# The last pair of heads after all five head fours, wider turned keys, and four more unread matmuls at the end of a decode kernel

## The chip, the core and the metric

The kernel runs on one core of one Trainium2 chip. The metric is the time of one execution on the device in microseconds (us), the median over several runs. Beside it there is the profile of one execution, whose clock starts at its first instruction; all points of time below are counted from there.

## What is computed

One decode step of a gated mix of two branches, for a batch of 8 with one new token each and a width of 576. Branch A is attention with cached keys and values (32 heads of width 128, 4096 positions); branch B is a small MLP.

```python
g = _sigmoid((x * gate_w).sum(-1, keepdims=True))
q = (x @ wq).reshape(B, Sq, H, Dh).transpose(0, 2, 1, 3)
scores = jnp.einsum("bhqd,bhkd->bhqk", q, k_cache) * (Dh ** -0.5)
p = _softmax(scores, axis=-1)
o = jnp.einsum("bhqk,bhkd->bhqd", p, v_cache)
a = o.transpose(0, 2, 1, 3).reshape(B, Sq, H * Dh) @ wo
b = _gelu(_layernorm(x) @ w1 + b1) @ w2 + b2
return g * a + (1 - g) * b
```

The keys and values are 268 MB each, in bf16, and everything is read once.

## The kernel before, in words

The work is cut into 32 groups (`NG`), each of 8 heads (`HB`) of one batch row. A group's keys lie over 128 partitions as 8 heads by 16 stretches of 256 positions. `scores` multiplies them by the query on VectorE (`mult`, L496), sums over the head width on TensorE against an identity matrix (L507 and, with weights that are already loaded, `held`, L180) and on VectorE (`reduce`, L515); `softmax` follows; `pv` (L556) multiplies probabilities by values, `evict` (L568) brings the sums to SBUF, and `gather` (L573) picks each head's rows out of them with the selection matrix `selO`, fp32, 8 columns wide. The order of each engine's instructions is written out by hand: the text order of the calls is the order in each engine's queue. The groups 1 to 30 are hardware loops on TensorE and VectorE; the start and the last group are written out straight. SyncE's queue issues all the large loads.

The change lies in the last group alone (`last`, 31), after its scores. Its values come in ten loads, `load_v_last` with the sizes of `V_LAST`; `v_part[i]` holds each one's pair of heads, its range and its landing.

- Parts 0 to 2 hold positions 0 to 159 of each stretch of 256, for all heads; `pv` works on them as on any group.
- Parts 3 to 9 hold the other 96 positions, ordered by pairs of heads: parts 3 and 4 are pairs 0 and 1 with 24 keys each per partition (`KW`), parts 5 and 6 are pair 2 with 16 and 8, and parts 7, 8 and 9 are the last pair with 8 each (256 KB a part).

`pv_turned` (L756) works on parts 3 to 9 with the roles turned: the values are the weights (128x128, one load each) and the probabilities the moving columns. For pairs 0 to 2 it streams 8 columns and adds onto what `gather` left in the bank `qb_ps`; for the last pair it streams 2 columns into the bank `o_ps[0]`. `norm_turned` (L763, result `v_A`) divides the heads of pairs 0 to 2 and writes them to `OT_sb`, which the projection reads; `norm_first` (L768) does so for the last pair's first positions; `norm_wide` (L772, result `v_B`) adds the last pair's turned part. `a_proj` projects with `wo`: per head four matmuls of 144 columns, one for each quarter of the output width, on 32 columns of the array each (`quarters`, L619). "Five fours" are five heads with four such matmuls each; the projection of this last group has 8 heads. L856 combines both branches, and one DMA writes the result. `keep_busy(n)` (L743 for the first, L180 for the others) issues n matmuls of 512 columns whose result nobody reads; they wait for nothing that is still under way at their place.

Before the change, the end of the last group ran in this order on TensorE: gather; parts 3, 4, 5, 6; part 7; projection of 4 heads; part 8; projection of 1 head; part 9; projection of 1 head; and, after `norm_wide`, of the last 2 heads.

Of the kernel before, what the change touches and what calls it, by code (L numbers as in the profile page):

```python
# [14 lines left out]
H = 32  # L15
# [7 lines left out]
HB = 8  # L23
# [11 lines left out]
TQ = 4  # L35
# [7 lines left out]
class Stream:  # L43
# [10 lines left out]
    def op(self, engine, fn, waits=(), dma=None, side=0):  # L54

        rec = [fn, [w for w in waits if w is not None], None, dma, (engine, side)]
        self.ops[engine].append(rec)
        if dma is not None:
            return ("dma", *dma)
        return ("op", engine, rec)  # L60
# [81 lines left out]
def bass_gated_mix__mha_block_cached__mixer_channel_mlp__decode_kernel(  # L142
# [18 lines left out]
    op = S.op  # L161

    def aside(engine, fn, waits=()):
        return op(engine, fn, waits, side=1)

    def pstride(t):
        return t[tuple([slice(None)] * len(t.shape))].ap[0][0]

    def view(t, offset, shape):
        ap = []  # L170
        stride = 1
        for n in reversed(shape[1:]):
            ap.insert(0, [stride, n])
            stride *= n
        return bass.AP(tensor=t, offset=offset, ap=[[pstride(t), shape[0]]] + ap)


    def held(e, out, lhsT, rhs, stop):

        return e.add_instruction(mybir.InstMatmult(  # L180
            name=nc.get_next_instruction_name(), engine=mybir.EngineType.PE,
            ins=[e.lower_ap(rhs), e.lower_ap(lhsT)], outs=[e.lower_ap(out)],
            start_tensor_calc=False, stop_tensor_calc=stop, tile_size=(128, 128), tile_position=(0, 0),
            ldweights=False))
# [15 lines left out]
    p1 = sb("p1", [128, 2, CT, DH], BF16)  # L200
# [36 lines left out]
    PW = view(p1, 2 * (FW + 3 * QN), [128, HB // 2, HB, (B * NHG - 8)])  # L237
# [9 lines left out]
    selO = sb("selO", [128, TQ, HB], F32)  # L247
# [19 lines left out]
    O_sb = sb("O_sb", [128, TQ, DH], F32)  # L267
# [5 lines left out]
    o_ps = bank[2:4]  # L273
    qb_ps = bank[4]
# [70 lines left out]
    NP = HB // 2  # L345
    KW = (NTT - T_ALL) // 4
# [21 lines left out]
    last = NG - 1  # L368
# [18 lines left out]
    def blank(ps):  # L387
# [17 lines left out]
    t = op("vector", lambda e: e.tensor_reduce(out=stat[:, 0:1], in_=x_sb, axis=AX.X, op=ALU.add), [ld_x])  # L405
    t1 = op("vector", lambda e: e.tensor_tensor_reduce(out=junk, in0=x_sb, in1=x_sb, scale=1.0, scalar=0.0,
                                                       op0=ALU.mult, op1=ALU.add, accum_out=stat[:, 1:2]))
    t = op("vector", lambda e: e.tensor_scalar(out=stat[:, 2:3], in0=stat[:, 0:1], scalar1=1.0 / D, scalar2=None,
                                               op0=ALU.mult), [t])
    t = op("vector", lambda e: e.tensor_tensor(out=stat[:, 3:4], in0=stat[:, 2:3], in1=stat[:, 2:3], op=ALU.mult), [t])  # L410
    t = op("vector", lambda e: e.scalar_tensor_tensor(out=stat[:, 6:7], in0=stat[:, 1:2], scalar=1.0 / D,
                                                      in1=stat[:, 3:4], op0=ALU.mult, op1=ALU.subtract), [t, t1])
# [30 lines left out]
    t = op("vector", lambda e: e.reciprocal(out=stat[:, 7:8], in_=stat[:, 5:6]), [a_sqrt])  # L443
# [8 lines left out]
    for half in range(2):  # L452
        for h in range(4):
            for kt in range(NKT):
                o = tr_ps[half][32 * h:32 * h + B, :]
                at = (kt * SK + half * (SK // 2) if kt < NKF else NKF * SK) + h * DH
                r = bass.AP(tensor=VB, offset=at, ap=[[pstride(VB), 128], [4 * DH, 4], [1, DH]])
                xi = kt if kt < NKF else NKF + half
                p_Q = aside("tensor", lambda e, o=o, r=r, kt=kt, xi=xi: e.matmul(
                    o, lhsT=xT_sb[:, xi, :], rhs=r, start=(kt == 0), stop=(kt == NKT - 1)),  # L460
# [8 lines left out]
    a_qb, v_mult, v_red, p_sum, v_nm, a_exp, v_P, p_pv, a_ev, p_oz, v_norm, v_rs, p_z, v_rz = ({} for _ in range(14))  # L469
# [99 lines left out]
                                                      func=ACT.Copy), [p_pv[n], p_oz.get(n - 1)])  # L569

    def gather(n, o, stop=True):
        for tt in range(TQ):
            p_oz[n] = op("tensor", lambda e, tt=tt: e.matmul(  # L573
                o, lhsT=O_sb[:, tt, :], rhs=selO[:, tt, :], start=(tt == 0), stop=(tt == TQ - 1 and stop)),
                [a_ev[n], v_norm.get(n - 1), c_selO] if tt == 0 else ())

    def norm(n):
# [37 lines left out]
    def quarters(t, n, j, w, first, stop, waits, end=aside):  # L615

        lhsT = bass.AP(tensor=t, offset=j, ap=[[pstride(t), 128], [n // BS, 32]])
        for i in range(4):
            last = (end if i == 3 else aside)("tensor", lambda e, i=i: e.matmul(  # L619
                y_ps[32 * i:32 * i + 32, 0:QN], lhsT=lhsT, rhs=w[:, i * QN:(i + 1) * QN], start=first, stop=stop),  # L620
                waits if i == 0 else ())
        return last
# [73 lines left out]
    def a_proj(h0, h1, normed):  # L696
        for h in range(h0, h1):
            st["p_a"] = quarters(OT_sb, H, h, wo_sb[:, h, :], h == H - HB, h == H - 1,
                                 [a_O[NG - 2], *normed, st["ld_wo3"], st["a_bx"]] if h == h0 else ())
# [38 lines left out]
    def keep_busy(n):  # L738

        for i in range(n):  # L740
            r = wo_sb[:, i, 0:512]
            if i == 0:
                fn = lambda e, r=r: e.matmul(tr_ps[1][:, :], lhsT=ident[:, :], rhs=r, start=True, stop=(n == 1))  # L743
            else:
                fn = lambda e, r=r, i=i: held(e, tr_ps[1][:, :], ident[:, :], r, i == n - 1)
            aside("tensor", fn, [v_red[last, NC - 1], st["ld_wo"]] if i == 0 else ())

    def pv_turned(n, i):
        g, t0, t1, land = v_part[i]
        for t in range(t0, t1):  # L750
            v = VL[:, T_ALL + g * KW + t, :]
            if g < NP - 1:
                o, p, start, stop = qb_ps[:, 0:HB], PW[:, g, :, t], False, (g, t) == (NP - 2, KW - 1)
            else:
                o, p, start, stop = o_ps[0][:, 0:2], PW[:, g, HB - 2:HB, t], t == 0, t == KW - 1
            p_oz[n] = op("tensor", lambda e, o=o, v=v, p=p, start=start, stop=stop: e.matmul(  # L756
                o, lhsT=v, rhs=p, start=start, stop=stop), [land, st["v_PW"]] if t == t0 else ())

# [3 lines left out]
    def norm_turned(n):  # L762
        return op("vector", lambda e: e.tensor_tensor(  # L763
            out=OT_b[:, n % B, H - HB:H - 2], in0=qb_ps[:, 0:HB - 2], in1=rz[:, 0:HB - 2], op=ALU.mult), [p_oz[n], v_rz[n]])

    def norm_first(n):

        v_norm[n] = op("vector", lambda e: e.tensor_tensor(  # L768
            out=X2[:, :], in0=qb_ps[:, HB - 2:HB], in1=rz[:, HB - 2:HB], op=ALU.mult), [p_oz[n], v_rz[n]])

    def norm_wide(n):
        return op("vector", lambda e: e.tensor_tensor(  # L772
            out=OT_b[:, n % B, H - 2:H], in0=o_ps[0][:, 0:2], in1=X2[:, :], op=ALU.add), [p_oz[n], v_norm[n]])
# [5 lines left out]
    for n in range(NG):  # L779
# [40 lines left out]
        pv(n - 1, v_land[n - 1], 0, NTT)  # L820
        evict(n - 1)
        gather(n - 1, oz_ps[:, 0:HB])
        if n < last:
            load_v(n)
# [15 lines left out]
    pv(last, v_part[2][3], *v_part[2][1:3])  # L840
    evict(last)
    keep_busy(3)
    gather(last, qb_ps[:, 0:HB], False)
    for i in range(3, 7):
        pv_turned(last, i)
    v_A = norm_turned(last)
    norm_first(last)
    pv_turned(last, 7)
    a_proj(H - HB, H - HB + 4, [v_A])
    pv_turned(last, 8)  # L850
    a_proj(H - HB + 4, H - HB + 5, [v_A])
    pv_turned(last, 9)
    v_B = norm_wide(last)
    a_proj(H - HB + 5, H - 2, [v_A])
    a_proj(H - 2, H, [v_B])
    t = op("vector", lambda e: e.scalar_tensor_tensor(  # L856
        out=out_sb[0:QP, :], in0=y_ps[0:QP, 0:QN], scalar=g4[0:QP, 0:1], in1=bmg_sb[0:QP, :],
        op0=ALU.mult, op1=ALU.add), [st["p_a"], st["g_bmg"]])
# [44 lines left out]
```

## Time and profile before

| | |
|---|---|
| median of 3 runs | 1297.49 us (1297.48 to 1297.62) |
| the profiled execution, its own time | 1297.77 us |
| its span, first to last instruction | 1295.7 us |
| mean granted TensorE clock | 0.829 of full |
| TensorE busy (matmul) | 58% of the span |
| VectorE busy | 66% |
| HBM read | 556.96 MB, 430 GB/s over the span |

In the profile, PE is TensorE's matmuls, PEld its weight loads, DVE is VectorE, ACT ScalarE, POOL GpSimd, and SP (SPq) SyncE's queue. "L756" is line 756 of the kernel. A line of the timeline gives the start, the length from the first start to the last end of a row of like instructions, engine, line, operation, operands, shapes and count; in brackets is how long the engine sat idle before and what ended that. PEclk is the granted TensorE clock, 1.00 being full.

### The profile page before, as it was taken

The numbers are of one execution on the slowest core, as the hardware profiler recorded it, in microseconds if no ns is written. First come the engines' busy times: TensorE is split into PE (matmuls) and PEld (weight loads), VectorE is DVE, ScalarE is ACT, GpSimd is POOL, SyncE is SP. The second block draws the span as 40 slices with busy tenths as digits, with TensorE's granted clock in tenths as the row PEclk, the third lists the DMA queues.
The fourth block names the chain that finished last, engine by engine and source line by source line (L and its number), as shares of the span: only waits on it lengthen the run. The fifth ranks groups of instructions, "written<-read, shape, count | busy, mean of one in ns | idle before, by whom it ended". The sixth has DMA issues, their size and how long they took to land.

```text
span 1295.7 us, 10767 instructions
## 1 busy us (share of the span) xinstructions
PE 745.8 (58%) x5042; PEld 155.4 (12%) x3247; DVE 851.9 (66%) x1083; ACT 69.7 (5%) x165; POOL 16.7 (1%) x29
## 2 busy tenths in 40 slices
PE   3865556555556555556555546645546655546657
PEld 1521111011111001111001111001111001111003
DVE  3656667766668766668766667766667776667772
ACT  3100000000000000000000000000000000000001
POOL 0010000000000000000000000000000000010000
PEclk8867898777889778888877888877789878789877
DMA  9999999999999999999999999999999999999998
GB/s 406 426 444 427 437 433 429 443 427 433 435 431 441 427 431 439 429 441 427 429 443 429 437 431 429 443 427 433 435 431 441 427 431 439 431 437 429 431 428 333
DMA packets 13283, 557.12 MB, mean 430 GB/s; under 512 B 1608, under 2 KB 2648, under 8 KB 3800
## 3 DMA queue, kind: packets, MB, share of 16 engines
q1 hardware_dynamic: 12996, 556.94, 99.6%
q8 instruction: 7, 0.11, 0.0%
q10 hardware_dynamic: 276, 0.04, 0.0%
q14 instruction: 4, 0.03, 0.0%
HBM read 556.96 MB, written 0.01 MB: 430 GB/s over the span
## 4 chain that ended last, share of the span: by engine, by line
DMA 68%; DVE 19%; PE 9%; issue 3%; SPq 0%; DVEq 0%
DMA KR<-in_A_k_cache_dram 67%; DVE p L496 17%; PE psb L180 7%; DVE s_sb L515 2%; DMA KR<-in_A_v_cache_dram 2%; PE psb L507 2%; SPq L285 0%; DVEq L135 0%; PE psb L619 0%; PE psb L756 0%; DVE out_sb L856 0%
## 5 line engine op out<-in xcount | busy, mean ns | idle before, releaser
L496 DVE TENSOR_TENSOR p<-KR,q_n 128x4096 bf16<-128x4096 bf16 x256 | 582.5, 2286 | 230.5 <-DMA KR<-in_A_k_cache_dram 230.5
L180 PE MATMUL psb<-p,ident 128*128 128x512 bf16 x1792 | 487.5, 418 | 0.0
L507 PE MATMUL psb<-p,ident 128*128 128x512 bf16 x256 | 111.7, 436 | 501.3 <-DVE p L496 501.2
L515 DVE TENSOR_REDUCE s_sb<-psb 128x32 f32<-128x512 f32 x256 | 175.2, 684 | 92.0 <-PE psb L180 92.0
L507 PEld LDWEIGHTS psb<-p,ident 128*128 128x128 bf16 x256 | 26.3, 103 | 951.2 <-DVE p L496 951.0
L556 PE MATMUL psb<-VB,P 128*32 128x512 bf16 x1984 | 112.7, 380 | 1.8 <-DMA VB<-in_A_v_cache_dram 1.8
L544 DVE TENSOR_SCALAR P<-E,own 128x256 bf16<-128x256 bf16 x248 | 51.4, 282 | 84.3 <-ACT E L541 84.3
L483 ACT ACTIVATE q_n<-q_bc 128x128 bf16<-128x128 bf16 x32 | 9.9, 309 | 867.7 <-DVE p L496 867.6
L556 PEld LDWEIGHTS psb<-VB,P 128*32 128x32 bf16 x1984 | 50.3, 97 | 49.8 <-DMA VB<-in_A_v_cache_dram 2.0
L573 PE MATMUL psb<-selO,O_sb 128*128 128x8 f32 x256 | 33.8, 258 | 21.8 <-ACT O_sb L568 21.8
L573 PEld LDWEIGHTS psb<-selO,O_sb 128*128 128x128 f32 x256 | 31.1, 191 | 37.8 <-ACT O_sb L568 37.8
L568 ACT ACTIVATE O_sb<-psb 128x512 f32<-128x512 f32 x32 | 19.1, 597 | 171.4 <-PE psb L556 171.4
L594 PE MATMUL psb<-yT_sb,KR 128*128 128x8 bf16 (+1 forms) x216 | 19.6, 229 | 0.0
L594 PEld LDWEIGHTS psb<-yT_sb,KR 128*128 128x128 bf16 (+1 forms) x216 | 18.4, 165 | 2.7 <-issue 1.4
L563 PEld LDWEIGHTS psb<-rs,ones 128*128 128x128 f32 x64 | 12.1, 190 | 45.8 <-issue 44.4
L541 ACT ACTIVATE E<-s_sb,mD 128x256 bf16<-128x256 f32 x32 | 16.0, 500 | 9.4 <-DVE mD L540 9.4
L648 POOL TENSOR_TENSOR Q<-Q,b 125x144 f32<-125x144 f32 x1 | 1.1, 1072 | 1067.3 <-DMA b<-in_B_b_dram 1067.3
L532 DVE TENSOR_REDUCE mA<-s_sb 128x1 f32<-128x256 f32 x32 | 13.4, 420 | 1.1
L547 DVE TENSOR_REDUCE es<-E 128x1 f32<-128x256 bf16 x32 | 13.2, 412 | 0.0
L488 ACT ACTIVATE OT_sb<-O_n 128x8 bf16<-128x8 bf16 x31 | 6.5, 208 | 83.2 <-DVE O_n L579 83.2
L578 DVE RECIPROCAL rz<-psb 128x8 f32<-128x8 f32 x31 | 6.2, 201 | 5.5 <-PE psb L573 5.5
L563 PE MATMUL psb<-rs,ones 128*128 128x8 f32 x64 | 9.2, 216 | 0.5 <-DVE O_n L579 0.5
(105 smaller groups left out, 134.1 us busy)
## 6 DMA issues: line engine op xcount, KB each, us to landing
KR<-in_A_k_cache_dram SPq DMA_DIRECT2D x2, 4096.0 KB, 27.2
VB<-in_A_v_cache_dram SPq DMA_DIRECT2D x1, 5376.0 KB, 20.8
VB<-in_B_w_dram SPq DMA_DIRECT2D x1, 5184.0 KB, 39.8
KR<-in_B_w_dram SPq DMA_DIRECT2D x1, 4608.0 KB, 43.2
VB<-in_A_wq_dram SPq DMA_DIRECT2D x1, 4096.0 KB, 12.5
KR<-in_A_v_cache_dram SPq DMA_DIRECT2D x2, 2048.0 KB, 13.9
KR<-in_A_wo_dram SPq DMA_DIRECT2D x1, 3456.0 KB, 24.8
VB<-in_A_v_cache_dram SPq DMA_DIRECT2D x1, 2816.0 KB, 38.8
```

What stands on the lines that cost most here:

```text
L180: return e.add_instruction(mybir.InstMatmult(name=nc.get_next_instruction_name(), engine=mybir.EngineType.PE, ins=[e.lower_ap(rhs), e.lowe ...
L496: v_mult[n, c] = op("vector", lambda e: e.tensor_tensor(out=p1[:, par, :, :], in0=k, in1=qb, op=ALU.mult), [k_land[n, s], a_q[n], p_sum.ge ...
L507: fn = lambda e, r=r: e.matmul(tr_ps[par][:, :], lhsT=ident[:, :], rhs=r, start=True, stop=False)
L515: v_red[n, c] = op("vector", lambda e: e.tensor_reduce(out=s_sb[:, at:at + CT], in_=tr_ps[par][:, :].rearrange("p (t c) -> p t c", c=CH), ...
L532: t = op("vector", lambda e: e.tensor_reduce(out=mA[:, 0:1], in_=s_sb[:, :], axis=AX.X, op=ALU.max), [v_red[n, NC - 1], c_mA])
L541: a_exp[n] = op("scalar", lambda e: e.activation(out=E[:, :], in_=s_sb[:, :], func=ACT.Exp, bias=mD[:, 0:1], scale=1.0), [v_nm[n], v_P.get ...
L544: v_P[n] = op("vector", lambda e, h=h: e.tensor_scalar(out=(P if n < NG - 1 else P_last)[:, :, h, :], in0=E[:, :].rearrange("p (q t) -> p ...
L556: p_pv[n] = op("tensor", lambda e, o=o, tq=tq, at=at, v=v: e.matmul(o, lhsT=(P if n < last else P_last)[:, tq, :, :].rearrange("p h t -> p ...
L563: p_z[n] = op("tensor", lambda e: e.matmul(oz_ps[:, HB:2 * HB], lhsT=ones[:, :], rhs=rs[:, :], start=True, stop=True), [v_rs[n], v_norm.ge ...
L568: a_ev[n] = op("scalar", lambda e: e.activation(out=O_sb[:].rearrange("p t d -> p (t d)"), in_=o_ps[n // last][:, :], func=ACT.Copy), [p_p ...
L573: p_oz[n] = op("tensor", lambda e, tt=tt: e.matmul(o, lhsT=O_sb[:, tt, :], rhs=selO[:, tt, :], start=(tt == 0), stop=(tt == TQ - 1 and stop)),
L594: st["p_up"] = (op if end else aside)("tensor", lambda e, w=w, o=o, kt=kt: e.matmul(o, lhsT=w, rhs=yT_sb[:, kt, :], start=(kt == 0), stop= ...
```

## The change

`gather` and `pv_turned` build the moving operand by hand, with a step of 0 that repeats the same columns: the last gather and the turned parts of pairs 0 to 2 stream their 8 columns four times (32 columns), those of the last pair their 2 columns sixteen times. The repeated columns land in columns of the bank that nobody reads. For all other groups the gather's operand is what it was. Two calls of `keep_busy(2)` are put in, behind part 3 and behind part 4. The projection of five heads comes right behind `norm_turned`, and parts 7, 8 and 9 follow it back to back; the projections of the last three heads stay behind them.

```diff
     def gather(n, o, stop=True):
+        k = o.shape[1] // HB
         for tt in range(TQ):
-            p_oz[n] = op("tensor", lambda e, tt=tt: e.matmul(
-                o, lhsT=O_sb[:, tt, :], rhs=selO[:, tt, :], start=(tt == 0), stop=(tt == TQ - 1 and stop)),
+            r = bass.AP(tensor=selO, offset=tt * HB, ap=[[pstride(selO), 128], *([[0, k]] if k > 1 else []), [1, HB]])
+            p_oz[n] = op("tensor", lambda e, tt=tt, r=r: e.matmul(
+                o, lhsT=O_sb[:, tt, :], rhs=r, start=(tt == 0), stop=(tt == TQ - 1 and stop)),
                 [a_ev[n], v_norm.get(n - 1), c_selO] if tt == 0 else ())
...
+    WS = 32
+
     def pv_turned(n, i):
+
         g, t0, t1, land = v_part[i]
+        p1s = pstride(p1)
         for t in range(t0, t1):
             v = VL[:, T_ALL + g * KW + t, :]
             if g < NP - 1:
-                o, p, start, stop = qb_ps[:, 0:HB], PW[:, g, :, t], False, (g, t) == (NP - 2, KW - 1)
+                o, h0, start, stop = qb_ps[:, 0:WS], 0, False, (g, t) == (NP - 2, KW - 1)
             else:
-                o, p, start, stop = o_ps[0][:, 0:2], PW[:, g, HB - 2:HB, t], t == 0, t == KW - 1
+                o, h0, start, stop = o_ps[0][:, 0:WS], HB - 2, t == 0, t == KW - 1
+            p = bass.AP(tensor=p1, offset=PW.offset + (g * HB + h0) * KW + t,
+                        ap=[[p1s, 128], [0, WS // (HB - h0)], [KW, HB - h0]])
...
     keep_busy(3)
-    gather(last, qb_ps[:, 0:HB], False)
-    for i in range(3, 7):
-        pv_turned(last, i)
+    gather(last, qb_ps[:, 0:WS], False)
+    pv_turned(last, 3)
+    keep_busy(2)
+    pv_turned(last, 4)
+    keep_busy(2)
+    pv_turned(last, 5)
+    pv_turned(last, 6)
     v_A = norm_turned(last)
     norm_first(last)
-    pv_turned(last, 7)
-    a_proj(H - HB, H - HB + 4, [v_A])
-    pv_turned(last, 8)
-    a_proj(H - HB + 4, H - HB + 5, [v_A])
-    pv_turned(last, 9)
+    a_proj(H - HB, H - HB + 5, [v_A])
+    for i in range(7, 10):
+        pv_turned(last, i)
     v_B = norm_wide(last)
     a_proj(H - HB + 5, H - 2, [v_A])
     a_proj(H - 2, H, [v_B])
```

## The prediction

> **What bounds the kernel now.** I read the page first, for its span and the shares of the chain that ended last; then the end of that chain, in order of time; then the timeline of the last ten microseconds, since the diff touches nothing earlier.
>
> ```profile
> span 1295.7 us, 10767 instructions
> ...
> DMA 68%; DVE 19%; PE 9%; issue 3%; SPq 0%; DVEq 0%
> ```
>
> ```profile
> 1269.20 21.12 DMA KR<-in_A_v_cache_dram
> 1290.32 0.05 issue
> 1290.36 0.37 PE psb L756 x8
> ```
>
> Two thirds of the span are transfers. The loads run ahead of the engines up to the last group, so all that this change can move is what lies behind the last values' landings. The chain says where that begins: part 7 (issued at 1269.20) lands at 1290.32, its eight turned matmuls start at 1290.36, 0.04 us behind the landing, and from there TensorE is named without a break.
>
> ```profile
> 1286.01 0.95 PE L573 MATMUL psb<-selO,O_sb 128*128 128x8 f32 x8
> 1286.82 0.78 PE L756 MATMUL psb<-p,KR 128*128 128x8 bf16 x24
> 1287.80 0.80 PE L756 MATMUL psb<-p,KR 128*128 128x8 bf16 x24 [0.19 <-DMA KR<-in_A_v_cache_dram]
> 1289.09 1.03 PE L756 MATMUL psb<-p,KR 128*128 128x8 bf16 x24 [0.49 <-DMA KR<-in_A_v_cache_dram]
> 1289.73 0.29 PEld L756 LDWEIGHTS psb<-p,KR 128*128 128x128 bf16 x8 [0.15 <-DMA KR<-in_A_v_cache_dram]
> 1290.16 0.17 DVE L763 TENSOR_TENSOR OT_sb<-psb,rz 128x6 bf16<-128x6 f32 x1 [9.82 <-PE psb L756]
> 1290.67 0.70 PE L619 MATMUL psb<-KR,OT_sb 128*32 128x144 bf16 x16
> 1291.31 0.37 PE L756 MATMUL psb<-p,KR 128*128 128x2 bf16 x8
> 1291.61 0.35 PE L619 MATMUL psb<-KR,OT_sb 128*32 128x144 bf16 x4
> 1291.89 0.37 PE L756 MATMUL psb<-p,KR 128*128 128x2 bf16 x8
> 1292.19 0.79 PE L619 MATMUL psb<-KR,OT_sb 128*32 128x144 bf16 x12
> 1292.30 0.16 DVE L772 TENSOR_TENSOR OT_sb<-psb,X 128x2 bf16<-128x2 f32 x1 [1.91 <-PE psb L756]
> 1292.51 0.21 PEld L619 LDWEIGHTS psb<-KR,OT_sb 128*32 128x32 bf16 x8 [0.18 <-DVE OT_sb L772]
> 1293.03 0.37 DVE L856 SCALAR_TENSOR_TENSOR out_sb<-psb,g,Q 125x144 bf16<-125x144 f32 x1 [0.57 <-PE psb L619]
> 1293.42 0.69 SPq L285 DMA_DIRECT2D out_dram<-out_sb  x1
> ```
>
> Parts 4, 5 and 6 wait for their landings (the brackets: 0.19, 0.49, 0.15 us), so up to 1290.16 the transfers set the pace. Parts 8 and 9 wait for nothing in brackets; they stand in TensorE's queue behind the projection. Part 9 starts at 1291.89. When did its values land?
>
> ```profile
> 1270.49 6.70 SPq L285 DMA_DIRECT2D KR<-in_A_v_cache_dram  x1
> KR<-in_A_v_cache_dram SPq DMA_DIRECT2D x1, 256.0 KB, 21.1
> ```
>
> This is the last of the ten loads: 1270.49 + 21.1 gives 1291.59. TensorE took it up 0.30 us later; that is the room for a new order. The TensorE clock is the second thing, read in stretches of 3.41 us whose borders are where the clock changes.
>
> ```profile
> core 0: us, PE busy (x), PEclk, DMA share, GB/s
> 1268.68:1272.09 3.41, 1.63 (x28) 1.00 0.81 344
> 1272.09:1275.51 3.42, 3.41 (x64) 1.00 1.01 426
> 1275.51:1278.92 3.41, 2.21 (x26) 1.00 1.00 420
> 1278.92:1282.33 3.41, 2.70 (x30) 0.50 0.98 410
> 1282.33:1285.74 3.41, 3.35 (x23) 0.50 1.01 414
> 1285.74:1289.16 3.42, 2.74 (x61) 1.00 1.02 388
> 1289.16:1292.57 3.41, 3.10 (x76) 0.50 0.23 87
> ```
>
> ```profile
> 1278.08 1.12 PE L556 MATMUL psb<-KR,p 128*32 128x512 bf16 x16
> L756 PE MATMUL psb<-p,KR x96: 165/175/193, 1286.8 to 1292.1; 128*128 128x8 bf16 x72, 128*128 128x2 bf16 x24
> ```
>
> In the first fence the clock is full or half, and it is half from 1289.16 to the end, where nothing hides TensorE any more. The two rows of the second fence are used below: where the wide matmuls of one stretch begin, and how long one turned matmul is (0.175 us).
>
> **The change part by part. The order.** `norm_turned` still starts at 1290.16, if part 6 isn't late (below), and ends at 1290.33. The projection's weight load follows VectorE by 0.05 us (L772 ends at 1292.46, the load starts at 1292.51), so the five heads start at 1290.38. Part 7, landed at 1290.32, now stands behind that wait, and parts 8 and 9 behind it; 0.06 us of TensorE are lost, at no cost, since the last landing comes later. Length of five heads at half clock: sixteen matmuls take 0.64 us up to the first of part 8 (1290.67 to 1291.31), four take 0.28 (1291.61 to 1291.89), so a head is 0.12 and twenty take 0.76, to 1291.14. Sixteen turned matmuls: 24 in 0.78 with a last one of 0.175 long means 0.026 from start to start, so parts 7 and 8 take 0.42, to 1291.56. Part 9 can't start before 1291.59 + 0.04 = 1291.63. So the new order just meets the last landing at half clock, with 0.07 us to spare, and by 0.4 us more at full clock. Part 9 then takes 0.37 as before, to 1292.00, and `norm_wide` starts 0.04 us behind (1291.89 + 0.37 = 1292.26 against 1292.30): at 1292.04 where it was 1292.30. **Term one: -0.26 us.** What is late next is the landing itself. No DMA and no instruction of ScalarE, GpSimd or SyncE changes its place, and the output's DMA still follows L856. The sixth head's four matmuls start beside `norm_wide` (0.21 us from its start to the next weight load) and stay hidden, as now.
>
> **The clock at the end.** Behind `norm_wide` lie 0.73 us (1292.30 to 1293.03): 0.21 to the weight load, two heads, the last matmul's own length, and VectorE.
>
> ```profile
> L619 PE MATMUL psb<-VB,hT_sb x144: 225/324/337, 73.7 to 77.7; 128*32 128x144 bf16 x144
> L619 PE MATMUL psb<-KR,OT_sb x32: 324/330/338, 1290.7 to 1292.6; 128*32 128x144 bf16 x32
> ```
>
> The first row is the MLP's down projection, the same shape; its shortest matmuls, 225 ns, are those behind a change to full clock, its median, 324, those at half. At full clock the last matmul is 0.105 shorter (330 to 225 ns), and the head in front of it takes 0.06 in place of 0.12. **Term two: -0.165 us, if the clock is full there.** Is it? Count how long columns stream in a stretch, at 0.228 us per 512 (below), 0.014 per 32. In 1268.68:1272.09 all 28 matmuls are wide ones, 1.63 us, and the clock stays full. In 1275.51:1278.92 the wide ones begin at 1278.08 and stream for 0.84, the others carry 8 columns: about 0.9, and it falls. In 1285.74:1289.16 an older unread matmul streams for 0.26, and 60 of 8 columns for 0.2: 0.46, and it falls, though the engine is counted busy for 2.74. So the border is between 0.9 and 1.63 us of streaming. The change makes this stretch 0.26 + 0.11 (gather) + 51 x 0.014 = 0.71 + 4 x 0.228 = 0.91: 2.0 us. It should stay full up to 1292.57, past the start of the last heads at about 1292.25.
>
> [...]
>
> **Wider streams.** No row has 32 columns behind a 128-column bf16 load; the nearest on both sides:
>
> ```profile
> 1249.21:1249.61 0.40, 0.40 (x9) 1.00 1.44 547
> 1249.21 0.40 PE L670 MATMUL psb<-Q,shift 128*128 128x64 bf16 x8
> 1279.16 0.50 PE L729 MATMUL psb<-E,q_bc 128*128 128x24 bf16 x12
> 1271.87 3.64 PE L556 MATMUL psb<-VB,P 128*32 128x512 bf16 x64 [1.78 <-DMA VB<-in_A_v_cache_dram]
> ```
>
> With 0.175 for the last one's length again, 64 columns at full clock are (0.40 - 0.175) / 7 = 0.032 apart, and 24 columns at half (0.50 - 0.175) / 11 = 0.030. Loads overlap streams in both, so I take about 0.027, as with 8 columns, and a cost of nothing; by 0.030 part 9 would be 0.03 longer. The other end is load and stream one after the other: 0.026 + 0.014 = 0.040 at full clock, 0.053 at half. In part 9 alone that is 7 x 0.014 = 0.10 or 7 x 0.027 = 0.19 us on the path; in parts 3 to 6 the waits for landings take it at full clock. Below nothing it can't be: more columns are streamed through the same loads. [...]
>
> **The unread matmuls.** At full clock 512 columns cost 0.228 (64 in four columns of the array, 16 rows of 0.228 in 3.64). Part 3's last one starts at 1287.43; two unread ones run from 1287.46 to 1287.91, part 4 starts 0.11 late and is through at 1288.55, two more end at 1289.01, and part 5 waits until 1289.09 anyway. [...] Without that cover (half clock, below) they cost 0.43 each.
>
> **Sum.** -0.26 - 0.165 = -0.42 us. The profiled execution took 1297.77 (1295.7 of span and 2.1 around it), so 1297.35 for it; it lies 0.28 over the median of the runs, 1297.49, and the median becomes 1297.07.
>
> **The rivals.** *The clock isn't moved* in the last stretch, because unread columns don't count for it or because the grid of 3.41 us falls elsewhere in other executions, which one profile can't show. For it: the rows give a border, not a rule. Against: 2.0 us is above every stretch that fell. [...] The order still pays: -0.26, 1297.23.
>
> *Slower: at half clock, the wide streams don't overlap their weight loads.* The place is parts 7 to 9, which no longer have the projection between them. The five heads end at 1291.14, sixteen at 0.053 end at 1291.99, past the landing; eight more with the last one's length take 0.56, and `norm_wide` starts at 1292.59, 0.29 later than now: 1297.78. It decides as soon as the starts there lie over (1292.26 - 0.175 - 1291.14) / 23 = 0.041 us apart with the clock at half. If the clock is half from 1286 on, the unread ones come on top:
>
> ```profile
> 1279.98 1.06 PE L180 MATMUL psb<-KR,ident 128*128 128x512 bf16 x2 [0.23 <-issue]
> ```
>
> Two of 0.63 in 1.06 are 0.43 apart. Part 3 would end at 1287.45, the first two at 1288.31, part 4 at 1288.94, the next two at 1289.80, parts 5 and 6 at 1290.43; the five heads would start 0.46 late, and `norm_wide` at 1292.42 even with overlap, 0.12 late. Against both: the rows at 24 and 64 columns, and a full clock at 1285.74 that the change doesn't touch.
>
> *Load and stream in series, but at full clock*: part 9 pays 0.10, -0.32, 1297.17.
>
> **How the numbers follow.** The forecast has a chance of 0.60, the clock that isn't moved 0.18, series at full clock 0.07, the slower end 0.11; 0.04 is left for executions that differ by something outside the tail. The range takes the forecast and, downwards, the 0.28 between two executions of one kernel, with 0.1 for the reading of the landings: 1296.7. Upwards it takes the slower end and the spread of the runs (0.14): 1297.9. 0.2% of this time, 2.6 us, is about what a measurement of this kernel can tell from no change, and every case stays within it: from the last landing to the output's issue at 1293.42 there are only 1.8 us to win, and what could be lost reaches 2.6 only where half clock from 1286 on and series come together (parts 3 to 6 then cost 2.54 instead of 1.26 beside the 1.72 of the unread ones, the five heads start at about 1292.75 and `norm_wide` near 1295.0, 2.7 late). So faster by more 0.02, within 0.95, slower by more 0.03, for that corner and for what lies outside the tail.
>
> **What would show it.** Right: in the timeline part 9's weight loads start at about 1291.63, 0.04 behind its landing, with a DMA wait in brackets; L772 near 1292.04; PEclk 1.00 from 1285.74 to the end; L619's last matmuls at 225 ns; L756's 24 in about 0.80; part 5 still waiting for its landing. Wrong: PEclk 0.50 behind 1289.16 (term two falls), L756 starts over 0.04 apart, or L763 later than 1290.2. Of the whole it would be wrong if the time moved by more than 1 us either way, which no row of the tail can pay for.

## The result, and the profile after

The changed kernel is slower: 1299.49 us (median of 22 runs, 1298.69 to 1301.9) beside 1297.82 of the kernel before (22 runs, 1297.4 to 1298.64) run beside it. The ratio of the means is 1.0016, with a 95% interval from 1.001 to 1.0023. It is within 0.2%, as forecast, but on the other side of zero and outside the range that the prediction gave. The profiled execution took 1299.64 us, with a span of 2.0 us more than before.

From the page of the kernel after, its span; then the end of its chain of waits (start, length, what):

```profile
span 1297.7 us, 10772 instructions
```

```profile
1266.11 18.16 DMA KR<-in_A_v_cache_dram
1284.27 0.04 issue
...
1286.71 1.44 PE psb L764 x24
```

Before, the last transfer on the chain landed at 1290.32. Now the transfers leave the chain at 1284.27, six microseconds earlier, and TensorE carries it from there: something on TensorE has become longer than the landings are apart. The timeline of the same stretch says what. (By the new line numbers L764 is `pv_turned`, L771 `norm_turned`, L780 `norm_wide`, L621 the projection, L745 and L180 the unread matmuls, L575 the gather, L866 the last sum.)

```profile
1285.63 1.08 PE L575 MATMUL psb<-selO,O_sb 128*128 128x32 f32 x8
1286.55 1.60 PE L764 MATMUL psb<-p,KR 128*128 128x32 bf16 x24
1288.20 0.38 PE L180 MATMUL psb<-KR,ident 128*128 128x512 bf16 x1
1288.42 1.60 PE L764 MATMUL psb<-p,KR 128*128 128x32 bf16 x24
1289.84 0.61 PE L745 MATMUL psb<-KR,ident 128*128 128x512 bf16 x1
1290.24 0.63 PE L180 MATMUL psb<-KR,ident 128*128 128x512 bf16 x1
1290.67 1.62 PE L764 MATMUL psb<-p,KR 128*128 128x32 bf16 x24
1292.32 0.17 DVE L771 TENSOR_TENSOR OT_sb<-psb,rz 128x6 bf16<-128x6 f32 x1 [11.16 <-PE psb L764]
1292.54 0.83 PE L621 MATMUL psb<-KR,OT_sb 128*32 128x144 bf16 x20 [0.26 <-DVE OT_sb L771]
1293.30 0.94 PE L764 MATMUL psb<-p,KR 128*128 128x32 bf16 x24
1294.28 0.16 DVE L780 TENSOR_TENSOR OT_sb<-psb,X 128x2 bf16<-128x2 f32 x1 [1.73 <-PE psb L764]
1295.02 0.37 DVE L866 SCALAR_TENSOR_TENSOR out_sb<-psb,g,Q 125x144 bf16<-125x144 f32 x1 [0.57 <-PE psb L621]
```

24 turned matmuls of pairs 0 to 2 take 1.60 us where they took 0.78. The last of them is 0.24 long, so their starts lie (1.60 - 0.24) / 23 = 0.059 us apart, against 0.026. The 24 of the last pair have 32 columns too, and take 0.94, or 0.032 apart. No turned matmul waits for a landing any more: of TensorE's rows only L621's has a bracket, and it waits for VectorE. (The weight load of part 4 still waits 0.18 us for its landing, beside the unread matmuls. The first of the four unread matmuls has no row in this trace; its place is the 0.29 us between the start of part 3's last matmul, 1287.91, and 1288.20.) The landing itself:

```profile
1270.80 6.69 SPq L285 DMA_DIRECT2D KR<-in_A_v_cache_dram  x1
KR<-in_A_v_cache_dram SPq DMA_DIRECT2D x1, 256.0 KB, 21.1
```

The last part lands at 1270.80 + 21.1 = 1291.90, 0.31 later than in the profile before. `norm_wide` starts 2.38 behind it; before it was 1292.30 - 1291.59 = 0.71. Of the 2.0 us of span, about 0.3 is when the values landed in this execution (part 2, where the chain now leaves the transfers, is as much later: 1284.32 beside 1284.03), and 1.67 is TensorE's work. That the medians differ by the same 1.67 is chance to the last digit, since each profile is of one execution. Last, the clock, on the same grid of 3.41 us:

```profile
1282.08:1285.49 3.41, 2.39 (x28) 1.00 1.01 416
1285.49:1288.90 3.41, 3.35 (x43) 1.00 1.02 392
1288.90:1292.31 3.41, 3.39 (x45) 0.50 0.31 114
```

It falls to half at 1288.90, although four unread matmuls were put in to hold it. Parts 4 to 6 show that the 0.060 doesn't come from the clock: starts are 0.060 apart on both sides of 1288.90.

### The profile page after: what moved, and what is told of

The parts are those of the page before. It is cut to its first block, busy times and chain, and to the rows that moved or that the text cites. A ratio compares the mean times of both kernels' runs of the same rounds, so it can differ in the third digit from the quotient of the medians.

```text
span 1297.7 us, 10772 instructions
## 1 busy us (share of the span) xinstructions
PE 746.2 (58%) x5045; PEld 157.2 (12%) x3249; DVE 852.1 (66%) x1083; ACT 69.6 (5%) x165; POOL 18.4 (1%) x29
## 4 chain that ended last, share of the span: by engine, by line
DMA 68%; DVE 19%; PE 10%; issue 3%; DVEq 0%; SPq 0%
DMA KR<-in_A_k_cache_dram 66%; DVE p L496 16%; PE psb L180 8%; DVE s_sb L515 2%; PE psb L507 2%; DMA KR<-in_A_v_cache_dram 1%; PE psb L764 0%; DVEq L135 0%; SPq L285 0%; PE psb L621 0%; PE psb L575 0%; PE psb L745 0%; PE psb L556 0%; DVE out_sb L866 0%; DVE OT_sb L771 0%
## 5 line engine op out<-in xcount | busy, mean ns | idle before, releaser
L180 PE MATMUL psb<-p,ident 128*128 128x512 bf16 x1792 | 485.9, 417 | 0.0
L575 PE MATMUL psb<-selO,O_sb 128*128 128x8 f32 (+1 forms) x256 | 33.9, 259 | 21.8 <-ACT O_sb L568 21.8
L575 PEld LDWEIGHTS psb<-selO,O_sb 128*128 128x128 f32 x256 | 31.0, 191 | 37.8 <-ACT O_sb L568 37.8
```

What stands on the lines that cost most here:

```text
L180: return e.add_instruction(mybir.InstMatmult(name=nc.get_next_instruction_name(), engine=mybir.EngineType.PE, ins=[e.lower_ap(rhs), e.lowe ...
L575: p_oz[n] = op("tensor", lambda e, tt=tt, r=r: e.matmul(o, lhsT=O_sb[:, tt, :], rhs=r, start=(tt == 0), stop=(tt == TQ - 1 and stop)), [a_ ...
```

## The experiments

My theory from these rows: the moving columns of the turned matmuls lie 48 bytes apart (24 keys of 2 bytes between two heads of a key), and reading 32 of them takes 0.060 us, which 8 of them (by that price an estimated 0.015) never showed, being under the 0.026 that those lay apart. Rivals: the unread matmuls; the order; or stream and load one after the other, or the repetition with a step of 0, whatever the distance.

### Taking the change apart

**Narrow streams.** Unread matmuls and order stay.

```diff
-                o, h0, start, stop = qb_ps[:, 0:WS], 0, False, (g, t) == (NP - 2, KW - 1)
+                o, h0, start, stop = qb_ps[:, 0:HB], 0, False, (g, t) == (NP - 2, KW - 1)
...
-                o, h0, start, stop = o_ps[0][:, 0:WS], HB - 2, t == 0, t == KW - 1
+                o, h0, start, stop = o_ps[0][:, 0:2], HB - 2, t == 0, t == KW - 1
...
-                        ap=[[p1s, 128], [0, WS // (HB - h0)], [KW, HB - h0]])
+                        ap=[[p1s, 128], [KW, HB - h0]])
...
-    gather(last, qb_ps[:, 0:WS], False)
+    gather(last, qb_ps[:, 0:HB], False)
```

> The changed kernel with the narrow streams of before (8 columns in the last gather and for pairs 0 to 2, 2 columns for the last pair); the new order and the four unread matmuls stay. Theory (the turned matmuls of 32 columns read keys that lie 48 bytes apart, and that read, 0.060 us each, is what makes the change slower): the starts of the turned matmuls are 0.026 to 0.027 us apart again, L771's first start falls back from 1292.3 to about 1290.5, and the time is that of the kernel before less 0.2 to 0.4 us. Rival (the four unread matmuls, 0.5 and 0.85 us in the changed kernel's trace, make it slower): still 1 us or more slower than before.

Measured: 1297.46 us (11 runs, two of them at 1298.81 and 1299.64, longer in their spans too), beside 1297.73 before; ratio 1.0, interval 0.9991 to 1.0009. From its timeline:

```profile
1288.08 0.80 PE L764 MATMUL psb<-p,KR 128*128 128x8 bf16 x24 [0.32 <-DMA KR<-in_A_v_cache_dram]
1290.41 0.16 DVE L771 TENSOR_TENSOR OT_sb<-psb,rz 128x6 bf16<-128x6 f32 x1 [9.32 <-PE psb L764]
1292.32 0.16 DVE L780 TENSOR_TENSOR OT_sb<-psb,X 128x2 bf16<-128x2 f32 x1 [1.68 <-PE psb L764]
```

The turned matmuls are back at 0.027 apart, part 4 waits for its landing again in spite of the unread ones in front of it, and by the median the whole loss is gone, as theory said. The loss needs the wide streams; whether their number of columns or the distance between these makes it, this run can't tell.

**No new unread matmuls.** Wide streams and order stay.

```diff
     pv_turned(last, 3)
-    keep_busy(2)
     pv_turned(last, 4)
-    keep_busy(2)
```

> The changed kernel without the four unread matmuls behind parts 3 and 4; wide streams and new order stay. Theory (the wide strided read): 72 turned matmuls at 0.060 take 4.3 us from about 1286.7, with a short wait for part 4, so norm_turned starts near 1291.3, about 0.9 behind the kernel before; time 0.5 to 1.0 us over before, about 1 us under the changed kernel. Rival (the unread matmuls): the loss is gone, 0.2 to 0.4 us under before.

Measured: 1298.99 us (11 runs, 1298.08 to 1299.92); ratio 1.0009, interval 1.0 to 1.0018.

```profile
1286.37 1.75 PE L575 MATMUL psb<-selO,O_sb 128*128 128x32 f32 x8
1287.94 4.47 PE L764 MATMUL psb<-p,KR 128*128 128x32 bf16 x72
1292.45 0.16 DVE L771 TENSOR_TENSOR OT_sb<-psb,rz 128x6 bf16<-128x6 f32 x1 [12.12 <-PE psb L764]
```

72 turned matmuls in one row of 4.47 us, with no wait among them. By the median the unread ones account for 0.5 of the loss beside wide streams, where I had expected about 1, and the wide streams for the rest. `norm_turned` is later here than I expected (1292.45, not 1291.3), because the gather took 1.75 us in this execution, not 1.08: the clock was at half ahead of it (two unread matmuls took 1.06 us there, 0.59 in the changed kernel's trace), and its fp32 weight loads go by the clock (0.97 us at full, 1.78 at half, below).

**The order alone.** Both of the above together: narrow streams, no new unread matmuls.

> Only the new order of the projection and of parts 7 to 9; narrow streams, no unread matmuls. Theory: part 9's first matmul starts 0.04 us behind its landing, norm_wide comes 0.26 us earlier against that landing than before, the clock at the end is as before; time 0.26 us under before (0.1 to 0.4). Rival (the order itself costs, since parts 7 to 9 start only behind the five heads): not faster than before, part 9 starting 0.2 us or more behind its landing.

Measured: 1297.32 us (11 runs, 1297.21 to 1297.85), beside 1297.73; ratio 0.9997, interval 0.9988 to 1.0006.

```profile
1270.91 6.51 SPq L285 DMA_DIRECT2D KR<-in_A_v_cache_dram  x1
KR<-in_A_v_cache_dram SPq DMA_DIRECT2D x1, 256.0 KB, 20.9
```

```profile
1290.36 0.17 DVE L771 TENSOR_TENSOR OT_sb<-psb,rz 128x6 bf16<-128x6 f32 x1 [9.93 <-PE psb L764]
1292.27 0.16 DVE L780 TENSOR_TENSOR OT_sb<-psb,X 128x2 bf16<-128x2 f32 x1 [1.68 <-PE psb L764]
```

The last landing is at 1270.91 + 20.9 = 1291.81 and `norm_wide` starts 0.46 behind it, 0.25 less than before (times to landing are given to 0.1 us). The median moved by 0.41; the interval still takes in no change. The spans, which leave out what lies around the program, are 1295.3 to 1295.7 us (median 1295.4) beside 1295.5 to 1296.1 (1295.7).

### What it is about the columns

**Heads side by side.** Everything as in the changed kernel, but the probabilities are laid out by key and then by head, so that the 8 columns of a matmul fill 16 bytes; the repetition to 32 stays.

```diff
-            d = bass.AP(tensor=p1, offset=PW.offset + i * KW, ap=[[pstride(p1), 128], [(HB + 2) * KW, NP], [1, KW]])
+            d = bass.AP(tensor=p1, offset=PW.offset + i, ap=[[pstride(p1), 128], [HB * KW + 2, NP], [HB, KW]])
...
-            p = bass.AP(tensor=p1, offset=PW.offset + (g * HB + h0) * KW + t,
-                        ap=[[p1s, 128], [0, WS // (HB - h0)], [KW, HB - h0]])
+            p = bass.AP(tensor=p1, offset=PW.offset + (g * KW + t) * HB + h0,
+                        ap=[[p1s, 128], [0, WS // (HB - h0)], [1, HB - h0]])
```

> The changed kernel with one thing different: the turned probabilities lie with the 8 heads of a key side by side (16 bytes) in place of 48 bytes apart; the reads still repeat to 32 columns, order and unread matmuls stay. Theory (the distance between the columns read is what costs): the starts are 0.027 to 0.032 us apart at full and at half clock, norm_turned is back near 1290.5, time 0.2 to 0.4 us under before. Rival (weight load and stream in series, or the repetition of columns by a step of 0, is what costs): 0.05 to 0.06 us apart as in the changed kernel, time 1.5 to 2 us over before.

Measured: 1297.92 us (11 runs, 1297.41 to 1298.65), beside 1297.73; ratio 1.0003, interval 0.9994 to 1.0012. The profiled execution took 1297.46.

```profile
1286.40 0.76 PE L764 MATMUL psb<-p,KR 128*128 128x32 bf16 x24
1287.94 0.77 PE L764 MATMUL psb<-p,KR 128*128 128x32 bf16 x24 [0.34 <-DMA KR<-in_A_v_cache_dram]
1291.75 0.27 PEld L764 LDWEIGHTS psb<-p,KR 128*128 128x128 bf16 x8 [0.34 <-DMA KR<-in_A_v_cache_dram]
1292.16 0.16 DVE L780 TENSOR_TENSOR OT_sb<-psb,X 128x2 bf16<-128x2 f32 x1 [1.66 <-PE psb L764]
1292.87 0.37 DVE L866 SCALAR_TENSOR_TENSOR out_sb<-psb,g,Q 125x144 bf16<-125x144 f32 x1 [0.55 <-PE psb L621]
```

```profile
1285.65:1289.07 3.42, 3.01 (x59) 1.00 1.01 386
1289.07:1292.48 3.41, 2.75 (x77) 1.00 0.25 92
```

The same 32 columns with the same repetition are 0.025 apart: neither the number of columns nor the step of 0 costs anything. The distance does, and without it 1.57 of the 1.67 us are gone. This execution is close to the one that the prediction drew: the clock stays full through 1292.48, part 9 waits for its landing (the weight load's bracket) and `norm_wide` follows 0.41 behind that load. But the median, 1297.92, is not the 0.2 to 0.4 us under the kernel before that I expected; other executions took longer, which the theory at that point didn't explain.

**Distances.** Pair 0 gets its heads 16 bytes apart, pair 1 8 bytes, pair 2 4 bytes, the last pair 16. At 48 bytes starts were 0.060 us apart, with the heads side by side 0.025. (This kernel and the next two have one execution each, for its rows.)

```diff
+    DIST = (8, 4, 2, 8)
...
+            m = DIST[g]
+            p = bass.AP(tensor=p1, offset=PW.offset + g * HB * KW + t // m * HB * m + h0 * m + t % m,
+                        ap=[[p1s, 128], [0, WS // (HB - h0)], [m, HB - h0]])
```

> A look, no timing: the changed kernel with the turned probabilities laid out so that the 8 heads of a key lie 16 bytes apart for pair 0 (part 3), 8 bytes for pair 1 (part 4), 4 bytes for pair 2 (parts 5 and 6), and the 2 heads of the last pair 16 bytes apart; 32 columns everywhere. [...] Rival (the cost grows with the distance): part 3 a third of the way, near 0.030, part 4 less. Rival (any step other than one element costs the same): 0.060 in all of parts 3 to 6.

```profile
1287.95 1.60 PE L769 MATMUL psb<-p,KR 128*128 128x32 bf16 x24
1290.20 0.95 PE L769 MATMUL psb<-p,KR 128*128 128x32 bf16 x24
1291.80 0.85 PE L769 MATMUL psb<-p,KR 128*128 128x32 bf16 x24
```

The clock is at half in all three rows (the unread matmuls between them are 0.59 to 0.63 us long; the changed kernel's at 1288.20, at PEclk 1.00, is 0.38). At 16 bytes 24 take 1.60, as at 48; at 8 bytes 0.95 (0.033 apart), at 4 bytes 0.85 (0.029, where 32 columns at 0.84 ns, 512 in 0.43, take 0.027 anyway). So at half clock a step of 4 bytes is as good as free, 8 nearly so, and 16 costs what 48 does: the two rivals, growth with distance and any step alike, fall.

**Widths.** As in the changed kernel, 48 bytes apart, with 16 columns in part 3, 64 in part 4, 32 in part 5, 128 in part 6. If the price goes by the column, the 0.060 of 32 columns makes 0.030 of 16, 0.120 of 64 and 0.240 of 128.

```diff
-    WS = 32
+    WS = 128
+    WIDE = {3: 16, 4: 64, 5: 32, 6: 128, 7: 64, 8: 16, 9: 32}
...
     def pv_turned(n, i):
-
+        WS = WIDE[i]
```

> A look, no timing: the changed kernel, heads 48 bytes apart as in it, with other numbers of repeated columns: the last gather 128, part 3 16, part 4 64, part 5 32, part 6 128, part 7 64, part 8 16, part 9 32. [...] Rival (a fixed price for each matmul whose columns lie apart): 0.055 or more in part 3 and far less than 0.24 in part 6.

```profile
1286.62 0.90 PE L766 MATMUL psb<-p,KR 128*128 128x16 bf16 x24
1288.09 2.88 PE L766 MATMUL psb<-p,KR 128*128 128x64 bf16 x24
1291.23 2.88 PE L766 MATMUL psb<-p,KR 128*128 128x32 bf16 x24
1292.17 0.62 PE L766 MATMUL psb<-p,KR 128*128 128x128 bf16 x2
1293.72 0.40 PE L766 MATMUL psb<-p,KR 128*128 128x128 bf16 x1
```

16 columns are (0.90 - 0.20) / 23 = 0.030 apart, 64 columns (2.88 - 0.29) / 23 = 0.113. The third row has parts 5 and 6 in one, 16 matmuls of 32 columns and 8 of 128; the last two rows are the first two and the last of part 6, so 128 columns are (1293.72 - 1292.17) / 7 = 0.221 apart, a little under that 0.240. The price is 1.7 to 1.9 ns for each column read, and no fixed price for the matmul.

**Heads in turn.** 48 bytes apart, 32 columns, but of 1 head in part 3, 2 in part 4, 4 in part 5, 8 in part 6, and 1 in part 8; the kernel leaves out the sums of the other heads.

```diff
+    TURN = {3: 1, 4: 2, 5: 4, 6: 8, 7: 2, 8: 1, 9: 2}
...
-                        ap=[[p1s, 128], [0, WS // (HB - h0)], [KW, HB - h0]])
+                        ap=[[p1s, 128], [0, WS // TURN[i]], [KW, TURN[i]]])
```

> A look, no timing: the changed kernel's layout (heads 48 bytes apart) and 32 columns, but the columns repeat 1 head in part 3, 2 heads in part 4, 4 heads in part 5, 8 in part 6, 1 head in part 8; the sums of the other heads are left out. In the changed kernel 8 in turn were 0.060 apart and 2 in turn 0.032. [...] Rival (it was the other bank or the shorter run of the last pair): part 4 0.060 while parts 7 and 9 stay at 0.032.

```profile
1286.49 0.90 PE L765 MATMUL psb<-p,KR 128*128 128x32 bf16 x24
1287.70 0.93 PE L765 MATMUL psb<-p,KR 128*128 128x32 bf16 x24
1288.99 1.56 PE L765 MATMUL psb<-p,KR 128*128 128x32 bf16 x24
```

At full clock (the unread matmuls between these rows are 0.38 us long) one head over and over is 0.031 apart (heads side by side took 0.025), two in turn 0.032, and parts 5 and 6 together (1.56 - 0.24) / 23 = 0.057. So two places in turn took little over half of what four and eight did together, and the last pair of the changed kernel was spared for that reason, not for its bank.

### Why executions of one kernel differ by one to three microseconds

**Side by side, no new unread matmuls** (the diffs of "No new unread matmuls" and "Heads side by side" together).

> The kernel with the 8 heads of a key side by side (16 bytes, wide streams, new order), but without the four unread matmuls behind parts 3 and 4. In the run with them the profiled execution was 0.2 us under the kernel before in its span, yet the runs spread from 1297.4 to 1298.65. Theory (the spread is the clock: where the grid of 3.41 us leaves TensorE at half clock from 1285 on, the unread matmuls take 0.43 each and stand in front of parts 4 and 5): without them the spread closes and the median is 0.3 to 0.4 us under before, like the order alone (1297.32). Rival (the wide streams bring the spread): it stays about 1.2 us wide.

Measured: 1297.46 us (11 runs, 1297.13 to 1298.39, ten of them up to 1297.72), beside 1297.76; ratio 0.9996, interval 0.9987 to 1.0005. The spread is mostly closed, by taking the unread ones away; the streams stayed wide. The spans say so more clearly, 1295.2 to 1295.6 us beside 1295.3 to 1296.5 with the unread ones: what makes the one run of 1298.39 long lies outside the program.

**Side by side, the four new ones kept, the seven older ones taken out.**

```diff
     spread_P(last)
-    keep_busy(3)
     pv(last, v_part[1][3], *v_part[1][1:3])
-    keep_busy(1)
...
     evict(last)
-    keep_busy(3)
```

> Heads side by side, wide streams, new order, the four new unread matmuls, but without the seven older unread matmuls (behind the spreading of the probabilities, behind part 1 and behind the eviction), so that the clock is more often at half when the gather begins. Theory: at half clock the gather takes 1.7 us in place of 0.9 and two unread matmuls 0.86, the turned matmuls 0.026 to 0.028 each as before; norm_turned comes about 1 us late and most runs are like the slow ones of the kernel with the older ones, 1298.3 to 1298.8. Rival (the clock does not set the spread): times as with the older ones, median 1297.9, 1297.4 the lowest.

Measured: 1298.13 us (11 runs, 1297.78 to 1298.92); ratio 1.0004, interval 0.9995 to 1.0013.

```profile
1285.85 1.92 PE L575 MATMUL psb<-selO,O_sb 128*128 128x32 f32 x8 [0.70 <-ACT O_sb L568]
1291.43 0.17 DVE L771 TENSOR_TENSOR OT_sb<-psb,rz 128x6 bf16<-128x6 f32 x1 [9.77 <-PE psb L764]
1292.93 0.16 DVE L780 TENSOR_TENSOR OT_sb<-psb,X 128x2 bf16<-128x2 f32 x1 [1.26 <-PE psb L764]
1293.55 0.37 DVE L863 SCALAR_TENSOR_TENSOR out_sb<-psb,g,Q 125x144 bf16<-125x144 f32 x1 [0.46 <-PE psb L621]
```

`norm_turned` comes 1.2 us later than with the older ones (1290.26 there), as expected, but the end gives 0.5 us of it back: the five heads took 0.54 us, as with the older ones at PEclk 1.00 (0.83 in the changed kernel, at half), and parts 7 to 9, which wait for no landing here, 0.77. The median rose by 0.2 only, and the lowest run by 0.4; four of the 11 runs, not most, lie at 1298.3 or above, and the runs still spread over 1.1 us. That falls between the theory and its rival: a half clock ahead of the gather costs time, but that it alone makes the spread isn't shown.

**The order alone, and no unread matmul at all** (the diff just above, on the order alone).

> Only the new order, narrow streams, and no unread matmul at all, older ones neither. Theory: at half clock the gather ends 0.8 us later, but parts 3 to 6 (72 matmuls at 0.027, 1.9 us) catch up with the landings of parts 5 and 6 before norm_turned, so the time stays that of the order alone within 0.3 us (1297.3 to 1297.6). Rival (the clock of the last ten microseconds carries the time whatever stands there): 1 us or more over before.

Measured: 1297.36 us (11 runs, 1297.19 to 1297.63), beside 1297.76; ratio 0.9996, interval 0.9987 to 1.0005.

```profile
1287.52 2.63 PE L764 MATMUL psb<-p,KR 128*128 128x8 bf16 x72
1292.04 0.16 DVE L780 TENSOR_TENSOR OT_sb<-psb,X 128x2 bf16<-128x2 f32 x1 [1.62 <-PE psb L764]
```

The gather took 1.88 us, as at half clock, and ended 1 us later than in the order alone, where it took 1.06, as at full; and the time is that of the order alone. With narrow streams, 72 turned matmuls need 1.9 us beside loads that take longer (2.63 us with the waits for landings), and the later gather is caught up before `norm_turned`. The older unread matmuls buy nothing that these runs can tell.

**The changed kernel without the seven older ones** (the diff on the heads side by side, here on the changed kernel).

> The changed kernel without the seven older unread matmuls, so that the clock is at half when the gather begins. Theory (the changed kernel's own runs, 1298.7 to 1301.9, differ by the clock between 1285 and 1290, since nothing is left there to take up a longer gather and longer unread matmuls): gather 0.8 us longer, each pair of unread ones 0.86, turned matmuls 0.060 as ever; norm_turned 1.5 to 1.8 us later than in the changed kernel's profile, median 1300.8 to 1301.5, as in its slow runs. Rival (the spread comes from elsewhere): the same mixture as the changed kernel, median 1299.5.

Measured: 1300.96 us (9 runs, 1300.79 to 1301.12), beside 1297.61; ratio 1.0025, interval 1.0015 to 1.0035.

```profile
1287.59 1.61 PE L764 MATMUL psb<-p,KR 128*128 128x32 bf16 x24
1289.85 1.62 PE L764 MATMUL psb<-p,KR 128*128 128x32 bf16 x24
1292.12 1.62 PE L764 MATMUL psb<-p,KR 128*128 128x32 bf16 x24
```

Between the ends of one row and the start of the next lie two unread matmuls at half clock (0.61 and 0.63 us long), part 3 starts 1.04 us later than in the changed kernel's profile and `norm_turned` 1.46 (1293.78). The spread has closed, at spans of 1298.8 to 1299.2 us. Of the changed kernel's 22 executions 15 have spans of 1296.6 to 1297.8, one 1298.4, and six 1299.1 to 1299.6, about where this kernel always is. That fits the theory: where TensorE has no slack before the last landing, the clock's state between 1285 and 1290 shows in the time. That each of those six was such an execution isn't shown; only one of the changed kernel's runs has a profile.

The best of these kernels are the order alone, 1297.32 and, without any unread matmul, 1297.36, each 0.4 us under before, in two separate sets of runs, and 2.1 to 2.2 us under the changed kernel. Each interval taken by itself still holds no change.

## Why the prediction was wrong, by its own steps

**Wider streams: this step failed.** It took 0.027 us between starts, with a worst end of 0.040 at full clock and 0.053 at half; measured were 0.060 at either. The rows that it leaned on, 24 and 64 columns, do show that loads and streams overlap, but their columns lie side by side in memory, while the turned ones lie 48 bytes apart, which the code says (`[KW, ...]`) and which I didn't set against them. With 8 columns the same read would by this price take 0.015 and hide under a load of 0.026, so no row of the turned matmuls could show it. The 72 matmuls of parts 3 to 6 became 0.033 longer each, 2.4 us, and the waits for landings that were to take that up held 0.83 (0.19, 0.49 and 0.15). The bounds were drawn around the wrong quantity: the number of columns, not where they lie.

By the runs the price of the distance sets in between 8 and 16 bytes (16 bytes 0.059, 8 bytes 0.033, 4 bytes 0.029, all at half clock), and it is less where two places take turns: 48 bytes apart they took 0.032, not 0.060.

**The unread matmuls: the cover was gone.** They were to cost nothing, with 0.08 us to spare (1289.01 to 1289.09), behind waits that the slower streams had already eaten. Without that they cost 0.5 us of the median (1299.49 against 1298.99). With quick streams the cover held in both profiles, and yet the medians differ: by 0.46 with the heads side by side (1297.92 against 1297.46; 0.3 by the spans) and by 0.14 with narrow streams (1297.46 against 1297.32, no more than such medians differ anyway). So a cost of nothing held in the executions that were profiled, not in the median. Half clock, at which the step itself gave 0.43 for each, is the likely reason: with the heads side by side and without the older unread matmuls, no wait is left in front of parts 4 and 5. It is argued, not shown, for the runs without a profile.

**Term two: the clock fell.** The count was 2.0 us of streaming in the stretch before 1289; the changed kernel's stretch 1285.49 to 1288.90 has 0.04 of an older unread matmul, 0.11 of the gather, 32 turned ones at 0.014 and two unread ones, 0.46: 1.1, since fewer matmuls fit into it. That is between the two ends of the border, 0.9 and 1.63, and the clock fell. So the rival that the clock isn't moved came true in this trace, for a reason that it didn't name. Where the streams were quick (heads side by side), the same count gives 0.09 + 48 x 0.014 + 0.91 = 1.7 and the clock held, as the step said. Its worth was too large even so. In that kernel the next border came at 1292.48, among the last matmuls, and `norm_wide` to the last sum took 0.71 in place of 0.73; without the older ones, where the last twelve projection matmuls took 0.68 us in place of 0.79, it took 0.62, so -0.11 us in place of -0.165.

**Term one: right.** It put `norm_wide` 0.45 us behind the last landing; the order alone has 0.46, with heads side by side part 9 waits for its landing in the trace. -0.26 forecast, -0.25 by the traces, to within the 0.1 us of a landing.

**The rivals.** The one on the slower side blamed the wide streams and had the sign, but its mechanism, load and stream in series at half clock (0.053), is refuted: 32 columns side by side are 0.025 apart at full clock and (0.85 - 0.19) / 23 = 0.029 at half (parts 5 and 6 with the heads side by side, without the older unread matmuls). Nor was its place right: the loss was decided not in parts 7 to 9 but in parts 3 to 6 (`norm_turned` started 2.16 us later than before, `norm_wide` 1.98), which it costed only in a far corner. There two of its numbers don't fit, either: 2.54 and 1.26 are for 48 matmuls, parts 3 to 6 have 72 (3.8 and 1.9), and its end point, 1292.75, goes by 72.

## What to carry to other kernels

Before a row is taken as the price of a new operand, compare how the operand lies in memory, not only its shape: a stream that is hidden under a weight load may be four times wider for nothing (0.025 us with the heads side by side), or not at all (0.060 at 48 bytes). Work added to keep a clock up is safe only while the waits that cover it last (0.83 us here, against 2.4 us of slower streams); recompute the cover after every other edit of the same change. And where the last transfer ends the chain, putting the independent work in front of the last landing's consumers is worth at most the gap between landing and take-up, here 0.30 us, less the 0.04 that the take-up itself took.

## What the runs showed of the hardware

- Reading moving columns of 2 bytes that lie 16 or 48 bytes apart took 1.7 to 1.9 ns a column; 32 columns 48 bytes apart took 0.060 us at full and at half TensorE clock alike. With only one or two places in turn, 48 bytes apart, it was about 1 ns (0.031 and 0.032 us for 32). Why two in turn are cheaper stays open.
- The gather's fp32 weight loads follow the clock: eight matmuls took 1.06 to 1.08 us at full and 1.88 to 1.92 at half, with 8 columns and with 32 alike. The eight loads by themselves took 0.97 and 1.78.
- Being counted busy doesn't hold the clock. Of the stretches of 3.41 us at full clock that are counted here, those with 0.5 to 1.1 us of streamed columns were followed by half clock, those with 1.6 us or more by full, whatever the busy time was (2.74 and 3.35 us ahead of half clock, 1.63 ahead of full). The kernel before narrows that: of four like stretches, each with the end of one group's `pv` and a gather, two with `pv` busy for 1.30 and 1.33 us (from 261.75 and 842.00) were followed by half clock, two with 1.42 and 1.43 (from 1074.12 and 493.86) by full. What exactly counts stays open; the 1.63 us are busy time of matmuls on a quarter of the array each.
